# Attention steps of the later tiles one position ahead, and the quarters of the norm's reciprocals at other positions

## The chip, the core and the metric

The kernel runs on one core of a Trainium2 chip. The metric is the time of one execution on the device, in microseconds (us). Before the change it is 1777.77 us, the median of three runs (1776.62 to 1777.86).

A core has TensorE (PE in the profile; its weight loads are PEld), VectorE (DVE), ScalarE (ACT), GpSimd (POOL) and SyncE (SP), which issues the transfers here. Each takes its own instructions in order, and they wait for each other by semaphores.

## The reference

All is float32. An attention over chunks of 64 tokens is followed by two gated layers; the second normalizes its input first.

```python
# q, k, v: (8, 8, 576, 64); chunks of 64 tokens, 9 to a sequence
scores = scale * np.matmul(q_c, k_c.transpose(0, 1, 2, 4, 3))
scores = scores - np.max(scores, axis=-1, keepdims=True)
attn = np.exp(scores)
attn = attn / (np.sum(attn, axis=-1, keepdims=True) + 1e-09)
out = np.matmul(attn, v_c)            # as x: 4608 tokens x 512

g = x @ w_gate                        # layer 1: 512 -> 1536
silu = g * (1.0 / (1.0 + np.exp(-g)))
x = silu * (x @ w_val) @ w_out        # 1536 -> 512

rms = np.sqrt(np.mean(x * x, axis=-1, keepdims=True) + 1e-06)
xn = x / rms * rms_g                  # layer 2, the same with xn
```

## The kernel before

Every product of layer 1 is made of three matmuls on values that are split into a high and a low part (`mm3`, lines 483 to 485): high by high, high by low, low by high. So a tile `x` comes as `xh` and `xl`, a hidden tile as `hh` and `hl`.

**Blocks, iterations, positions.** The tokens form 9 blocks of 512 (0 to 8). In layer 1 a block has 12 iterations, one for each 128 of the 1536 hidden features. An iteration has three stretches on PE of 12 matmuls each: `g` (`emit_g`), `v` (`emit_v`) and `y` (`emit_y`), where `y` multiplies the hidden tile of the iteration before by its output weights. Behind each stretch stands a place for other work, so a block has 36 places, called positions: position 3f is behind `g` of iteration f, 3f + 1 behind `v`, 3f + 2 behind `y`. A table `at` holds what is emitted at each (`put`), counted from a block's start, and the main loop calls `run(0)`, `run(1)`, `run(2)`. Each engine's queue then has its instructions in the order in which they were emitted.

**The chain of a hidden tile.** After `g`, ACT takes the tanh (L495) and DVE makes the product `sg` of the gate (L496, which ends the use of `g`'s PSUM bank). After `v`, DVE multiplies by `v` (L512, which ends the use of `v`'s bank; there is one bank for `g` and one for `v`), ACT rounds to `hh` (L515), and DVE makes `hl` (L517), which `y` of the next iteration needs in its second matmul. In the program L512 of an iteration is emitted ahead of position 3f + 2, L496 behind position 3f, and L517 at the start of the next iteration, ahead of its `g`: on DVE whatever was emitted at position 3f + 2 stands ahead of this `hl`.

**Attention.** There are 36 tiles of 128 tokens (0 to 35); a tile is needed a block after its attention is made. From tile 8 on, the steps of tile i stand around a = `score_at(i)`, counted from the start of block 0, and e = `score_at(i + 1)`:

- at a - 1, `trans_att`: two transpositions on DVE into `qT` and `kT` (L328);
- at a, `att_both(i - 1)`: on PE, the second product of tile i - 1 (16 matmuls, L441, from `pT`) and the scores of tile i (16 matmuls, L345, from `qT` and `kT`), both of 64x64, into the PSUM tile `both`;
- at a + 1 and a + 2, `att_m` and `att_n`: maximum and difference on DVE (L364, L365), exponential on ACT, sum and reciprocal on DVE (L378 to L382), a multiplication on POOL (L383), which makes `p`;
- at e - 4 and e - 3, `att_td`: two halves of a transposition of `p` into `pT` on DVE (L399, eight instructions of 32x128 each);
- at e, `att_both(i)`, and at e + 1, `att_lo(i)`: DVE makes `xl` of the tile (L477).

The loads of the chunks that come later (`load_qk`, `load_v`) are spread over positions that are counted from a - 1.

**The rest in blocks 1 to 8.** The norm of the block before: squares and their sum on POOL (L562 to L568), a sum by PE at position 17 (L586, L587), a square root on ACT, its reciprocal on DVE in four quarters of 128x128 (`rms_rec`, L600), a Newton step at position 27 (L605 to L609) and four multiplications from position 28 on (`rms_x`, L617). From block 1 to the start of block 7 the weights of layer 2 are also converted, one at each of positions 7, 13, 19, 25, 31 and 1 (of the next block): three instructions on DVE, L128, L131 and L136 (the trio, below), then sums and differences on POOL and roundings on ACT (L185 to L191). In the first iteration of a block, DVE and ACT also copy `y` of the block before out of PSUM (L548, L550).

```python
    def score_at(i):
        n = i - 8
        return NP + (8 * n if n < 4 else 32 + 9 * (n - 4))   # NP = 36
```

So from tile 12 on the steps repeat every 9 positions, four tiles to a block: `att_both` stands at positions 5, 14, 23 and 32 of a block, the halves of `att_td` at 1, 2, 10, 11, 19, 20, 28 and 29, and `trans_att` at 4, 13, 22 and 31. The quarters of the reciprocal stand at 19, 21, 23 and 25.

Of the kernel before, what the change touches and what calls it, by code (L numbers as in the profile page):

```python
# [19 lines left out]
def tile_kernel(  # L20
# [270 lines left out]
    def trans_tok(i, tags=None):  # L291
        ts_ = []
        both = ps_pair("a", f"qkP{i}") if tags is None else None
        pts = []
        for z, nm in enumerate("qk"):
            t = tok[i][z]
            if both is None:
                pt = ps.tile([P, HP, P], F32, tag=tags[z], name=f"{nm}P{i}")
            else:
                pt = both[:, z].rearrange("p (h q) -> p h q", h=HP)  # L300
            for hp in range(HP):
                nc.tensor.transpose(
                    pt[:, hp, :], t[:, 2 * hp:2 * hp + 2, :].rearrange("p a b -> p (a b)"), ident
                )
            pts.append(pt)
        for z, nm in enumerate("qk"):
            if i < NW // P:
                sb = spare_tile([P, HP, P], f"{nm}T{i}")
            else:
                sb = att.tile([P, HP, P], F32, tag=f"{nm}T", name=f"{nm}T{i}")  # L310
            nc.scalar.copy(sb, pts[z])
            ts_.append([sb[:, hp] for hp in range(HP)])
        qkT[i] = ts_
# [7 lines left out]
    def trans_att(i):  # L321
        ts_ = []
        for z, nm in enumerate("qk"):
            t = att.tile([P, HP, P], F32, tag=f"{nm}T", name=f"{nm}T{i}")
            tv = t.rearrange("p a (b c) -> p a b c", c=32)
            (g0, n0), (g1, n1) = where[2 * i], where[2 * i + 1]
            if g0 == g1:
                nc.vector.transpose(out=tv, in_=gt[g0][z][:, :, 2 * n0:2 * n0 + 4, :])  # L328
            else:
                nc.vector.transpose(out=tv[:, :, 0:2], in_=gt[g0][z][:, :, 2 * n0:2 * n0 + 2, :])  # L330
                nc.vector.transpose(out=tv[:, :, 2:4], in_=gt[g1][z][:, :, 2 * n1:2 * n1 + 2, :])
            ts_.append([t[:, hp] for hp in range(HP)])
        qkT[i] = ts_
# [22 lines left out]
    def att_m(i):  # L356
        sb = score.pop(i)
        m = att.tile([P, 2, HP], F32, tag="m", name=f"m{i}")
        if i < NW // P:
            pt = spare_tile([P, HP, 2, CH], f"p{i}")  # L360
        else:
            pt = att.tile([P, HP, 2, CH], F32, tag="p", bufs=2, name=f"p{i}")
        s3 = sb.rearrange("p z (h c) -> p z h c", h=HP)
        nc.vector.tensor_reduce(out=m, in_=s3, op=ALU.max, axis=AX.X)  # L364
        nc.vector.tensor_tensor(  # L365
            out=pt.rearrange("p h z c -> p z h c"),
            in0=s3,
            in1=m.rearrange("p z (h o) -> p z h o", o=1).to_broadcast([P, 2, HP, CH]),
            op=ALU.subtract,
        )  # L370
        nc.scalar.activation(pt, pt, AF.Exp, scale=SCALE)
        prob[i] = pt

    def att_n(i):
        pt = prob[i]
        r = att.tile([P, HP * 2, 1], F32, tag="r", name=f"r{i}")
        p8 = pt.rearrange("p a b c -> p (a b) c")
        nc.vector.tensor_reduce(  # L378
            out=r.rearrange("p a o -> p (a o)"), in_=p8, op=ALU.add, axis=AX.X
        )  # L380
        nc.vector.tensor_scalar_add(r, r, 1e-9)
        nc.vector.reciprocal(out=r, in_=r)  # L382
        nc.gpsimd.tensor_tensor(  # L383
            out=p8, in0=p8, in1=r.to_broadcast([P, HP * 2, CH]), op=ALU.mult
        )
# [3 lines left out]
    def att_td(i, c):  # L389
        pt = prob[i]  # L390
        if c == 0:
            probT[i] = att.tile([P, HP, P], F32, tag="pT", name=f"pT{i}")
        pT = probT[i]
        for a in range(2):
            r = (2 * c + a) * 32
            for z in range(2):
                for b in range(2):
                    o = (2 * z + b) * 32
                    nc.vector.transpose(  # L399
                        out=pT[o:o + 32, :, r:r + 32], in_=pt[r:r + 32, :, z, b * 32:b * 32 + 32]  # L400
                    )
# [61 lines left out]
    def att_both(i):  # L463
        both = ps_pair("a", f"both_{i}")
        if i >= 2 * NW // P:
            att_pv(i, i * P // NW, xb=both[:, :, :HP * CH], put_off=True)
        if i + 1 < NT_:
            att_s(i + 1, sb=both[:, :, HP * CH:])
        if i >= 2 * NW // P:
            att_hi(i, i * P // NW)  # L470

    def att_lo(i, j):
        xb = xps.pop(i)
        xh, xl = x_tiles(0, j)
        o = i * P - blocks[j][0]
        ah, al = (t[:, :, o:o + P].rearrange("p h (c q) -> p c h q", c=2) for t in (xh, xl))
        nc.vector.tensor_sub(al, xb, ah.bitcast(F32))  # L477
# [118 lines left out]
    def rms_rec(j, z):  # L596
        n = blocks[j][1] // 4
        ms, r = rms[j]
        a = slice(z * n, (z + 1) * n)
        nc.vector.reciprocal(out=r[:, a], in_=r[:, a])  # L600
# [22 lines left out]
    def tiles_of(j):  # L623
        t0, n = blocks[j]
        return list(range(t0 // P, (t0 + n) // P))
# [4 lines left out]
    NP = 3 * NF  # L630

    def put(l, j, pos, fn):
        at.setdefault((l * NB + j) * NP + pos, []).append(fn)
# [11 lines left out]

    def score_at(i):
        n = i - 8
        return NP + (8 * n if n < 4 else 32 + 9 * (n - 4))

    for x, (l, j) in enumerate(seq):  # L650
        if x + 1 < len(seq):
            nl, nj = seq[x + 1]
            if nl == 0:
                for n, i in enumerate(tiles_of(nj)):
                    if i >= 8:
                        a = score_at(i)
                        e = score_at(i + 1)
                        b = a - 1 - x * NP
                        if i == 8:
                            put(0, 0, a, lambda: att_both(7))  # L660
                        put(0, 0, a - 1, lambda i=i: trans_att(i))
                        put(0, 0, a + 1, lambda i=i: att_m(i))
                        put(0, 0, a + 2, lambda i=i: att_n(i))
                        put(0, 0, e - 4, lambda i=i: att_td(i, 0))
                        put(0, 0, e - 3, lambda i=i: att_td(i, 1))
                        put(0, 0, e, lambda i=i: att_both(i))
                        put(0, 0, e + 1, lambda i=i, nj=nj: att_lo(i, nj))
                    else:
                        b = (0, 9, 18, 27)[n]
                        put(l, j, b, lambda i=i: trans_tok(i))  # L670
                        put(l, j, b + 2, lambda i=i: att_s(i))
                        put(l, j, b + 3, lambda i=i: att_m(i))
                        put(l, j, b + 4, lambda i=i: att_n(i))
                        put(l, j, b + 6, lambda i=i: att_t(i))
                        put(l, j, b + 7, lambda i=i, nj=nj: att_pv(i, nj))
                        put(l, j, b + 8, lambda i=i, nj=nj: att_lo(i, nj))
                    for c in (2 * i, 2 * i + 1):
                        g = where[c][0]
                        if g > 0 and c == groups[g][-1] and g + 2 < len(groups):
                            dq, dv, nq = {4: (21, 18, 10), 7: (3, 9, 12), 8: (8, 12, 12)}.get(i, (1, 11, 8))  # L680
                            spread(l, j, b + dq, nq, lambda g=g: load_qk(g + 2))
                            spread(l, j, b + dv, 3, lambda g=g: load_v(g + 2))
        if x > 0 and seq[x - 1][0] == 0:
            pj = seq[x - 1][1]
            for d in range(KD):
                put(l, j, 3 + 2 * d, lambda pj=pj, d=d: rms_sq(pj, d))
            put(l, j, 14, lambda pj=pj: rms_split(pj))
            put(l, j, 17, lambda pj=pj: rms_mm(pj))
            for z in range(4):
                put(l, j, 19 + 2 * z, lambda pj=pj, z=z: rms_rec(pj, z))  # L690
            put(l, j, 27, lambda pj=pj: rms_newton(pj))
            for d in range(KD):
                put(l, j, 28 + 2 * d, lambda pj=pj, d=d: rms_x(pj, d))
# [286 lines left out]
    with tc.manual_schedule():  # L980
# [151 lines left out]
        pj = NB - 1  # L1132
# [111 lines left out]
```

## Time and profile before

| what | value |
|---|---|
| median of three runs | 1777.77 us |
| the profiled execution's own time | 1777.3 us |
| its span, first to last instruction | 1775.5 us |
| PE busy | 1740.8 us, 98% of the span |
| PEld busy | 1468.2 us, 83% |
| DVE busy | 1260.3 us, 71% |
| ACT busy | 672.4 us, 38% |
| POOL busy | 394.6 us, 22% |
| layer 1, blocks 2 to 7 | from 249.9 to 887.8 us of the span |

The profile is of one execution. A page of it gives the busy time of each engine, a chain of waits and the costliest groups of instructions; the trace behind it can be asked for a stretch (busy time of each engine and PE's granted clock), for the waits of an engine, added up by who ended them, and for the instructions of an engine in order of time. Matmuls overlap: one of 512 columns is shown with 0.39 us, but the next starts sooner, so the time that PE needs is read from start to start. A time in brackets behind an instruction, [1.52 <-DVE hl L517], says how long its engine had been idle before it and what ended that.

### The profile page before, as it was taken

To read this page: it belongs to the slowest core of one execution; us is meant where nothing else is said; L and a number is where in the kernel's file an instruction comes from. 1 tells how busy PE (TensorE), PEld (TensorE's weight loads), DVE (VectorE), ACT (ScalarE), POOL (GpSimd) and SP (SyncE) were. 2 spreads that over 40 slices of the span, in tenths; PEclk is the share of its full clock that TensorE was granted. 3 is DMA by queue.
4 is the path that set the end of the run, shared out by engine and by line. 5 is a ranking of instruction groups with operands and counts; after the bars stand their busy time and mean duration, and the time that the engine had idled before them with its cause. 6 is when DMAs were issued, how large, how long until landed. Compare 5 with 4: busy or idle time off the path is not lost.

```text
span 1775.5 us, 28911 instructions
## 1 busy us (share of the span) xinstructions
PE 1740.8 (98%) x10086; PEld 1468.2 (83%) x10086; DVE 1260.3 (71%) x2250; ACT 672.4 (38%) x1248; POOL 394.6 (22%) x391
## 2 busy tenths in 40 slices
PE   7999999999999999999999999999999999999998
PEld 5788878777788787778888888888888888999998
DVE  6996776977878777785735566955794478568566
ACT  6772323223332332323122334623452345345343
POOL 1002244243342534242031200200120011002000
PEclk8999999999999999999999999999999999999999
DMA  9997777776777766773335476687678768987986
GB/s 218 316 261 198 208 217 198 218 197 203 217 210 215 218 203 203 218 211 126 117 120 202 137 238 195 200 258 218 194 211 247 211 188 223 299 271 226 312 254 177
DMA packets 451457, 379.73 MB, mean 214 GB/s; under 512 B 275696, under 2 KB 302320, under 8 KB 451312
## 3 DMA queue, kind: packets, MB, share of 16 engines
q1 hardware_dynamic: 449712, 377.68, 72.1%
q8 instruction: 81, 1.33, 0.3%
q14 instruction: 64, 0.52, 0.1%
q10 hardware_dynamic: 1600, 0.20, 0.1%
HBM read 316.41 MB, written 61.34 MB: 213 GB/s over the span
## 4 chain that ended last, share of the span: by engine, by line
PE 83%; DVE 8%; SPq 3%; DMA 2%; issue 2%; ACT 1%; POOL 1%; ACTq 0%; DVEq 0%; POOLq 0%
PE g L483 5%; PE g L485 4%; PE g L484 4%; PE v L483 4%; PE v L484 4%; PE v L485 4%; PE y L484 2%; PE y L485 2%; PE y_b L484 2%; PE y_b L483 2%; PE y_b L485 2%; PE y L483 2%; DVE pT L399 2%; SPq L317 2%; PE ygA L484 1%
## 5 line engine op out<-in xcount | busy, mean ns | idle before, releaser
L515 ACT CAST hh<-sg 128x512 fp32r<-128x512 f32 x108 | 67.1, 621 | 375.2 <-DVE sg L512 375.2
L483 PE MATMUL g<-xh,wg 128*128 128x512 f32 x432 | 173.1, 401 | 1.8 <-DVE sg L496 1.1
L483 PE MATMUL v<-xh,wv 128*128 128x512 f32 x432 | 169.9, 393 | 3.7 <-DVE sg L512 2.7
L484 PE MATMUL g<-xl,wg 128*128 128x512 f32 x432 | 169.5, 392 | 0.0
L485 PE MATMUL g<-xh,lg 128*128 128x512 f32 x432 | 169.4, 392 | 0.0
L485 PE MATMUL v<-xh,lv 128*128 128x512 f32 x432 | 168.2, 389 | 0.0
L484 PE MATMUL v<-xl,wv 128*128 128x512 f32 x432 | 168.2, 389 | 0.0
L881 POOL TENSOR_TENSOR h<-h,h 128x512 f32<-128x512 f32 (+1 forms) x30 | 37.1, 1235 | 521.2 <-DVE h L859 521.2
L496 DVE SCALAR_TENSOR_TENSOR sg<-sg,g 128x512 f32<-128x512 f32 x108 | 73.3, 679 | 107.7 <-ACT sg L495 107.7
L399 DVE STREAM_TRANSPOSE pT<-p 32x128 f32<-32x128 f32 x448 | 135.5, 302 | 6.1
L495 ACT ACTIVATE sg<-g 128x512 f32<-128x512 f32 x108 | 64.4, 597 | 168.4 <-PE g L485 167.9
L917 DVE TENSOR_TENSOR hl<-h,hh 128x512 fp32r<-128x512 f32 (+1 forms) x180 | 121.7, 706 | 6.0 <-ACT hh L916 5.9
L916 ACT CAST hh<-h 128x512 fp32r<-128x512 f32 (+1 forms) x180 | 100.4, 577 | 47.2 <-PE yvA L485 20.0
L383 POOL TENSOR_TENSOR p<-p,r 128x512 f32<-128x512 f32 x36 | 40.3, 1121 | 340.7 <-DVE r L382 273.5
L840 DVE TENSOR_TENSOR sgt<-sgt,sig 128x512 f32<-128x512 f32 (+1 forms) x90 | 58.3, 648 | 74.1 <-ACT sig L839 74.0
L839 ACT ACTIVATE sig<-sgt 128x512 f32<-128x512 f32 (+1 forms) x90 | 53.2, 591 | 147.4 <-DVE sgt L847 147.3
L517 DVE TENSOR_TENSOR hl<-sg,hh 128x512 fp32r<-128x512 f32 x108 | 88.0, 815 | 25.8 <-ACT hh L515 24.7
L483 PEld LDWEIGHTS v<-xh,wv 128*128 128x128 f32 x432 | 81.1, 188 | 23.3 <-DVE sg L512 5.2
L483 PEld LDWEIGHTS g<-xh,wg 128*128 128x128 f32 x432 | 81.6, 189 | 21.4 <-DVE sg L496 2.3
L485 PEld LDWEIGHTS g<-xh,lg 128*128 128x128 f32 x432 | 81.6, 189 | 17.5
L484 PEld LDWEIGHTS g<-xl,wg 128*128 128x128 f32 x432 | 81.7, 189 | 16.6 <-DVE xl L477 0.4
L485 PEld LDWEIGHTS v<-xh,lv 128*128 128x128 f32 x432 | 81.1, 188 | 17.1
(806 smaller groups left out, 4684.7 us busy)
## 6 DMA issues: line engine op xcount, KB each, us to landing
wrg<-w_scratch SPq DMA_DIRECT2D x210, 256.0 KB, 3.3
wrv<-w_scratch SPq DMA_DIRECT2D x210, 256.0 KB, 3.4
wro<-w_scratch SPq DMA_DIRECT2D x210, 256.0 KB, 3.2
lg<-lo_scratch SPq DMA_DIRECT2D x96, 256.0 KB, 2.9
lv<-lo_scratch SPq DMA_DIRECT2D x96, 256.0 KB, 3.2
lo<-lo_scratch SPq DMA_DIRECT2D x96, 256.0 KB, 4.0
w_scratch<-wsg SPq DMA_DIRECT2D x42, 256.0 KB, 2.6
w_scratch<-wsv SPq DMA_DIRECT2D x42, 256.0 KB, 2.7
```

Source lines behind the costliest of these rows:

```text
L399: nc.vector.transpose(out=pT[o:o + 32, :, r:r + 32], in_=pt[r:r + 32, :, z, b * 32:b * 32 + 32])
L483: nc.tensor.matmul(o, sh, mh, start=first, stop=False, skip_group_check=free)
L484: nc.tensor.matmul(o, sh, ml, start=False, stop=False, skip_group_check=free)
L485: nc.tensor.matmul(o, sl, mh, start=False, stop=last, skip_group_check=free)
L495: nc.scalar.activation(sg[:, :n], g[:, :n], AF.Tanh, scale=0.5)
L496: return sg, lambda: nc.vector.scalar_tensor_tensor(out=sg[:, :n], in0=sg[:, :n], scalar=1.0, in1=g[:, :n], op0=ALU.add, op1=ALU.mult)
L515: nc.scalar.copy(hh[:, :n], sg[:, :n])
L517: return product, lambda: nc.vector.tensor_sub(hl[:, :n], sg[:, :n], hh[:, :n].bitcast(F32))
L839: nc.scalar.activation(sg[:, :tw], src[:, :tw], AF.Sigmoid)
L840: nc.vector.tensor_mul(t[:, :tw], src[:, :tw], sg[:, :tw])
L916: nc.scalar.copy(hh[:, :tw], src)
L917: nc.vector.tensor_sub(hl[:, :tw], src, hh[:, :tw].bitcast(F32))
```

## The change

From tile 12 on, every step of a tile's attention moves one position ahead: the table's second branch begins at 31 in place of 32. `att_both` then stands at positions 4, 13, 22 and 31, behind `v` in place of behind `y`; the halves of `att_td` at 0, 1, 9, 10, 18, 19, 27 and 28; `trans_att` at 3, 12, 21 and 30; `att_m`, `att_n` and `att_lo` move with them, and so do the spread loads of these tiles. The last steps of tile 11 (`att_td`, `att_both`, `att_lo`), which are counted from the next tile, move too. The quarters of the reciprocal go from 19, 21, 23 and 25 to 20, 21, 23 and 26. Nothing is added or taken away: PE, DVE, ACT and POOL have the same instructions.

```diff
     def score_at(i):
         n = i - 8
-        return NP + (8 * n if n < 4 else 32 + 9 * (n - 4))
+        return NP + (8 * n if n < 4 else 31 + 9 * (n - 4))
...
             for z in range(4):
-                put(l, j, 19 + 2 * z, lambda pj=pj, z=z: rms_rec(pj, z))
+                put(l, j, (20, 21, 23, 26)[z], lambda pj=pj, z=z: rms_rec(pj, z))
```

**DVE, iterations 0 and 1 of a block.** The names carry block and iteration (`hl_5_0` is of block 5, iteration 0; the last number is the program's own). Before:

```order
L496 SCALAR_TENSOR_TENSOR sg_5_0_6531<-sg_5_0_6531,g_5_0_6518 128x512
L399 STREAM_TRANSPOSE pT_6557<-p_6458 32x4x32 x8
L128 TENSOR_SCALAR cmo_1_6570<-w64o_1_6348 128x512
L131 SCALAR_TENSOR_TENSOR cmo_1_6570<-w64o_1_6348,cmo_1_6570 128x512
L136 SCALAR_TENSOR_TENSOR cro_1_6537<-cro_1_6537,cmo_1_6570 128x512
L512 SCALAR_TENSOR_TENSOR sg_5_0_6531<-v_5_0_6541,sg_5_0_6531 128x512
L550 COPY ysb_0_4_6588<-y_4_1_5490 128x512
L550 COPY ysb_0_4_6589<-y_4_b 128x512
L399 STREAM_TRANSPOSE pT_6557<-p_6458 32x4x32 x8
L517 TENSOR_TENSOR hl_5_0_6555<-sg_5_0_6531,hh_5_0_6554 128x512
L496 SCALAR_TENSOR_TENSOR sg_5_1_6630<-sg_5_1_6630,g_5_1_6617 128x512
L328 STREAM_TRANSPOSE qT_6660<-xq_5821 128x512
```

And with the change:

```order
L399 STREAM_TRANSPOSE pT_6537<-p_6436 32x4x32 x8
L496 SCALAR_TENSOR_TENSOR sg_5_0_6535<-sg_5_0_6535,g_5_0_6522 128x512
L399 STREAM_TRANSPOSE pT_6537<-p_6436 32x4x32 x8
L128 TENSOR_SCALAR cmo_1_6582<-w64o_1_6352 128x512
L131 SCALAR_TENSOR_TENSOR cmo_1_6582<-w64o_1_6352,cmo_1_6582 128x512
L136 SCALAR_TENSOR_TENSOR cro_1_6550<-cro_1_6550,cmo_1_6582 128x512
L512 SCALAR_TENSOR_TENSOR sg_5_0_6535<-v_5_0_6554,sg_5_0_6535 128x512
L550 COPY ysb_0_4_6600<-y_4_1_5526 128x512
L550 COPY ysb_0_4_6601<-y_4_b 128x512
L517 TENSOR_TENSOR hl_5_0_6568<-sg_5_0_6535,hh_5_0_6567 128x512
L328 STREAM_TRANSPOSE qT_6636<-xq_5803 128x512
L328 STREAM_TRANSPOSE kT_6638<-xk_5804 128x512
```

The first half of L399 now stands ahead of the gate's product L496, the second half ahead of the trio and no longer between the copies and `hl`; the transpositions L328 (`qT`, then `kT`) now stand straight behind `hl`, where the next L496 stood between before.

**DVE, iteration 6 of a block.** Before:

```order
L496 SCALAR_TENSOR_TENSOR sg_5_6_7137<-sg_5_6_7137,g_5_6_7124 128x512
L399 STREAM_TRANSPOSE pT_7171<-p_7039 32x4x32 x8
L600 RECIPROCAL rr_7107<-rr_7107 128x128
L128 TENSOR_SCALAR cmv_1_7189<-w64v_1_6927 128x512
L131 SCALAR_TENSOR_TENSOR cmv_1_7189<-w64v_1_6927,cmv_1_7189 128x512
L136 SCALAR_TENSOR_TENSOR crv_1_7151<-crv_1_7151,cmv_1_7189 128x512
L512 SCALAR_TENSOR_TENSOR sg_5_6_7137<-v_5_6_7155,sg_5_6_7137 128x512
L399 STREAM_TRANSPOSE pT_7171<-p_7039 32x4x32 x8
L517 TENSOR_TENSOR hl_5_6_7169<-sg_5_6_7137,hh_5_6_7168 128x512
```

And with the change:

```order
L399 STREAM_TRANSPOSE pT_7143<-p_7009 32x4x32 x8
L496 SCALAR_TENSOR_TENSOR sg_5_6_7141<-sg_5_6_7141,g_5_6_7128 128x512
L399 STREAM_TRANSPOSE pT_7143<-p_7009 32x4x32 x8
L128 TENSOR_SCALAR cmv_1_7200<-w64v_1_6931 128x512
L131 SCALAR_TENSOR_TENSOR cmv_1_7200<-w64v_1_6931,cmv_1_7200 128x512
L136 SCALAR_TENSOR_TENSOR crv_1_7164<-crv_1_7164,cmv_1_7200 128x512
L512 SCALAR_TENSOR_TENSOR sg_5_6_7141<-v_5_6_7168,sg_5_6_7141 128x512
L600 RECIPROCAL rr_7111<-rr_7111 128x128
L517 TENSOR_TENSOR hl_5_6_7182<-sg_5_6_7141,hh_5_6_7181 128x512
L328 STREAM_TRANSPOSE qT_7245<-xq_6404 128x512
```

The first quarter of the reciprocal went from ahead of the trio and L512 to behind L512; the second half of L399 went from behind L512 to ahead of the trio.

**PE, iteration 1 of a block.** With the change:

```order
L485 MATMUL v_5_1_6648<-xh_5_5499,lv_5_1_6446 128x512
L441 MATMUL both_6664<-pT_6537,xv_5542 64x64 x16
L345 MATMUL both_6664<-kT_6638,qT_6636 64x64 x16
L483 MATMUL y_5_0_6707<-hh_5_0_6567,wo_0_460 128x512
L484 MATMUL y_5_0_6707<-hl_5_0_6568,wo_0_460 128x512
```

Before, L441 and L345 stood behind the twelve matmuls of `y`; now they stand between `v` and `y`.

## Rows read from the trace of the kernel before

**Rows 1.** Busy time by stage, blocks 2 to 7: start:end, length, engines, PEclk, DMA, GB/s.

```profile
249.00:888.00 639.00, 627.84 (x4114) 510.68 (x4113) 487.44 (x968) 194.13 (x371) 230.88 (x254) 1.00 0.68 198
```

**Rows 2.** Waits of PE in blocks 1 to 7: us in total, times, longest us.

```profile
PE y L484 <- DVE hl L517: 9.6, 7, 1.5
PE v L483 <- DVE sg L512: 2.7, 6, 0.8
PE g L483 <- DVE sg L496: 0.7, 2, 0.4
```

**Rows 3.** PE in time, block 5, iteration 1: start us, us, instruction, [idle before].

```profile
580.45 0.39 PE L483 MATMUL v<-xh,wv 128*128 128x512 f32 x1
...
583.17 0.39 PE L483 MATMUL y<-hh,wo 128*128 128x512 f32 x1
585.08 0.50 PE L484 MATMUL y<-hl,wo 128*128 128x512 f32 x1 [1.52 <-DVE hl L517]
...
587.52 0.40 PE L485 MATMUL y_b<-hh,lo 128*128 128x512 f32 x1
...
588.94 0.50 PE L483 MATMUL g<-xh,wg 128*128 128x512 f32 x1
```

**Rows 4.** PE in time, block 5, iteration 7, last of g and last of y.

```profile
634.19 0.39 PE L485 MATMUL g<-xh,lg 128*128 128x512 f32 x1
...
640.64 0.39 PE L485 MATMUL y_b<-hh,lo 128*128 128x512 f32 x1
```

**Rows 5.** DVE in time, block 5, iterations 0 and 1.

```profile
573.18 0.69 DVE L496 SCALAR_TENSOR_TENSOR sg<-sg,g 128x512 f32<-128x512 f32 x1 [2.99 <-ACT sg L495]
...
578.19 0.68 DVE L512 SCALAR_TENSOR_TENSOR sg<-v,sg 128x512 f32<-128x512 f32 x1
...
581.23 2.52 DVE L399 STREAM_TRANSPOSE pT<-p 32x128 f32<-32x128 f32 x8
583.78 1.24 DVE L517 TENSOR_TENSOR hl<-sg,hh 128x512 fp32r<-128x512 f32 x1
...
585.55 0.70 DVE L328 STREAM_TRANSPOSE qT<-xq 128x512 f32<-128x512 f32 x1
586.18 0.66 DVE L328 STREAM_TRANSPOSE kT<-xk 128x512 f32<-128x512 f32 x1
...
588.10 0.69 DVE L517 TENSOR_TENSOR hl<-sg,hh 128x512 fp32r<-128x512 f32 x1 [0.69 <-ACT hh L515]
```

**Rows 6.** DVE in time, block 5, iterations 6 and 7.

```profile
628.42 0.69 DVE L496 SCALAR_TENSOR_TENSOR sg<-sg,g 128x512 f32<-128x512 f32 x1 [3.43 <-ACT sg L495]
...
631.54 0.95 DVE L600 RECIPROCAL rr<-rr 128x128 f32<-128x128 f32 x1
632.41 0.36 DVE L128 TENSOR_SCALAR cmv<-w64v 128x512 uint32<-128x512 uint32 x1
...
634.21 0.69 DVE L512 SCALAR_TENSOR_TENSOR sg<-v,sg 128x512 f32<-128x512 f32 x1
...
637.49 0.69 DVE L517 TENSOR_TENSOR hl<-sg,hh 128x512 fp32r<-128x512 f32 x1
```

**Rows 7.** PE in time, block 1: a tile's att_both that stands behind v.

```profile
190.22 0.39 PE L485 MATMUL v<-xh,lv 128*128 128x512 f32 x1
190.53 0.69 PE L441 MATMUL both<-pT,xv 64*64 64x64 f32 x32
191.05 0.65 PE L345 MATMUL both<-kT,qT 64*64 64x64 f32 x32
191.63 0.50 PE L483 MATMUL y<-hh,wo 128*128 128x512 f32 x1
```

**Rows 8.** POOL in time, block 5, iteration 1: its first work since block 4.

```profile
578.35 0.74 POOL L185 TENSOR_TENSOR wto<-cro,cro 128x256 f32<-128x256 f32 x1 [8.91 <-DVE cro L136]
```

**Rows 9.** DVE in time, block 5, iteration 2: the trio beside POOL, to the next product.

```profile
594.46 0.80 DVE L128 TENSOR_SCALAR cmg<-w64g 128x512 uint32<-128x512 uint32 x1
...
598.08 0.68 DVE L512 SCALAR_TENSOR_TENSOR sg<-v,sg 128x512 f32<-128x512 f32 x1
```

## The prediction

> **What bounds the kernel now.** I read first the busy time by stage. In blocks 2 to 7 PE is busy 627.84 of 639.00 us [rows 1], so it is the bound and what can be won there is what it waits, not its work; its granted clock is 1.00 of full (2.4 GHz), so nothing is to be won from the clock. Then the waits of PE [rows 2]: three lines stand in blocks 1 to 7. `y` waits for `hl` seven times (six times in blocks 2 to 7, some 1.5 each, and once in block 1), `v` waits six times for the product L512 that frees its bank, `g` twice for L496. All three are released by DVE. Then PE in order of time, to see what one wait costs with the slower start behind it. Twelve matmuls of `v` take 583.17 - 580.45 = 2.72 [rows 3], 0.2267 each. From the first matmul of `y` to its twelfth should take 11 x 0.2267 = 2.49; it takes 587.52 - 583.17 = 4.35. So **iteration 1 of a block loses 1.86**. In iteration 7, from the last of `g` to the last of `y` are 24 matmuls, 5.44; the rows show 640.64 - 634.19 = 6.45 [rows 4]. So **iteration 7 loses 1.01**.
>
> Last, DVE in order of time, to see why it is late. At a block's start it idles 2.99 before L496 (573.18), and then works without a longer pause through half a transposition, the trio, L512, two copies and the other half, which runs from 581.23 to 583.78; only then comes `hl`, until 585.02 [rows 5], while `y` could have used it in its second matmul at 583.40. At iteration 6 it idles 3.43 before L496, then come half a transposition, a quarter of the reciprocal, the trio and L512 at 634.21 [rows 6], while `v` wants its bank at 634.19 + 0.23 = 634.42. So DVE is late at two places of a block and idle just before both. The first loss stands in blocks 2 to 7 (six times), the second in blocks 2 to 6 (five times: the trio at position 19 ends with block 6, and so does the wait).
>
> **The change, part by part.** I replay DVE with the durations of the rows, in the new order, on the old clock of block 5.
>
> *Block start.* The first half of L399 moves ahead of L496, where 2.99 of idle time is free and the half takes 2.5. L496 still starts at 573.18, when ACT has its tanh. Behind it comes the second half, where the first stood, so the trio, L512 (578.19) and the copies stay where they are. `hl` starts at 581.23 in place of 583.78. It takes 0.69 where nothing disturbs it and took 1.24 here [rows 5], so it ends between 581.92 and 582.47, and `y`, which wants it at 583.40 or later, doesn't wait. **1.86 goes, six times: 11.2.**
>
> *What is late next there.* `att_both` now stands ahead of `y` and wants `qT` and `kT`. They follow `hl` on DVE: 586.18 - 585.55 = 0.63 for the first, 0.66 for the second [rows 5], less some 0.07 by which DVE starts ahead of a reported end (0.70 against 0.63). So `kT` is there at 583.14, or at 583.69 behind a slow `hl`. The scores want it at 583.17 + 0.08 (a step of 0.31 in place of 0.23 before L441) + 0.52 = 583.77 [rows 7]. The margin is 0.63, or 0.08. I take no wait, and keep the slow end for a rival.
>
> *Iteration 6.* The first half of L399 moves into the 3.43 of idle time before L496; the second stands behind L496. The quarter of the reciprocal, which held the trio back from 631.54 to 632.41, moves behind L512. So the trio starts at 631.54, 0.87 earlier, and L512 at 633.34. It ends at 634.03, 0.39 before `v` wants the bank. Behind L512 stand the quarter, until 634.8, and the cast on ACT, some 0.7 behind the product's end (0.69 before the undisturbed `hl` [rows 5]); `hl` runs from 634.8 to 635.5, and `y` wants it at 637.4. `kT` is there at 636.7, and wanted at 637.74 (634.42, the 2.72 of `v`, and 0.60 as above). **1.01 goes, five times: 5.05.**
>
> *`att_both` behind `v`.* A tile of block 1 whose step already stands there costs 191.63 - 190.22 - 0.23 = 1.18 [rows 7]; behind `y` it costs 588.94 - 587.52 - 0.23 = 1.19 [rows 3]. Nothing.
>
> *Block 1.* It holds what is left of [rows 2]: one wait of `g` at iteration 9 for L496 behind the Newton step, one at iteration 7, and one each of `v` and `y` in iteration 10. The half transposition moves there too, but the Newton step stays. I take about half of the two waits of `g` with their slow starts: **0.5**. Bounds: nothing, and all of them, 0.8 + 0.7 + 0.5 and three slow starts of 0.34 (1.86 less the 1.52 of the wait [rows 3]), 3.0.
>
> *Loads, POOL, the other quarters.* The spread loads go one position ahead with their tiles on SP's queue. PE waits for no transfer in these blocks [rows 2], and the transfers are no more; nothing. POOL's multiplication of `p` moves with L382, its distance to L399 stays three positions; were POOL late, the half transposition would hold L496 up, and `g` wants its bank only behind `v` and `y`, 5.44 later. The other quarters stay or go back by one position, to places where DVE next waits for PE; the Newton step comes one position behind the last in place of two, with the same 5.44 for `g`'s bank behind it. Nothing.
>
> **The sum.** 11.2 + 5.05 + 0.5 = 16.7. Against the profiled execution, 1777.3, that is 1760.6; the median of the runs is 0.5 above it, so **1761.0**. A measurement of this kernel can tell about 0.2%, 3.6 us, from no change.
>
> **A rule against it.** `hl` took 1.24 beside POOL in place of 0.69 [rows 5], and POOL starts a run of work behind the trio, at 578.35, with 0.74 an operation [rows 8]. The Trainium skill, page "SBUF — State Buffer", section "SBUF: two separate sides", says that VectorE with two SBUF inputs and GpSimd take a shared port pair as an exclusive lock for a whole instruction, the other fully blocked. By that `hl` could take 0.69 + 0.74 = 1.43 (an estimate from that page and the rows); the trace shows less, 1.24. By the rule `kT` would come 0.11 late, with a slow start 0.45 a block, and the sum would be 14.0, which gives 1763.8; it is one way into the first rival below.
>
> **The rivals.**
>
> *The wait moves to `kT`.* If copies and `hl` come as little as 0.1 later than replayed with a slow `hl`, the scores wait in iteration 1. For it: the margin of 0.08. Against: `hl` 2.55 earlier meets POOL at another operation. Price: up to the 0.55 that a slow `hl` adds, and a slow start of 0.34, so 0.9 in six blocks, 5.3: up to 1766.3; with half of the 0.55, 3.7 and 1764.7.
>
> *Iteration 7 keeps its wait.* The margin of `v`'s bank is 0.39. If the trio starts that much later, because the half transposition does not fit before L496, the five waits stay: 5.05, so 1766. Against: 3.43 of idle time for 2.5.
>
> *The wait only changes its name.* If DVE's idle time before L496 can't be used, since `p` is not ready one position earlier, all stays as late as it is: 1777. Against: POOL makes `p` three positions ahead.
>
> *Slower: the trio meets POOL.* In iteration 2 the trio takes 598.08 - 594.46 = 3.62 beside POOL [rows 9], in iteration 6 only 634.21 - 632.41 = 1.80 [rows 6]. If the new order lets POOL's work fall on the trio of iterations 0 and 6, each is 1.82 longer: `kT` comes at 583.69 + 1.82 = 585.51, 1.74 late and with a slow start 2.1; L512 ends at 635.85, 1.43 late, with a slow start 1.8. That is 3.9 a block for the 2.87 that goes: five times 1.0 and 0.2 in block 7, so some 5 slower, 1782.5. It decides once the trio is longer by about 1.3 at both places (kT late by 1.2 and the bank by 0.9, with two slow starts 2.8). Against: POOL is idle for 8.91 until that trio's own L136 releases it [rows 8].
>
> **How the numbers follow.** The forecast 0.72, `kT` 0.14, iteration 7 0.07: all faster, 0.93. The wait that changes its name 0.04: same. The trio 0.03: slower. The likeliest is 1761.0. The forecast's own range is 1758.5 (all of block 1's waits gone, 2.5 more) to 1763; the range that holds the first three cases reaches up to 1766.5, and leaves out 0.07.
>
> **What would show it.** In blocks 2 to 7 the waits of `y` for `hl` and of `v` for L512 are gone, a block takes 2.9 less, and PE is idle under 2 us in these blocks in place of 11 [rows 1]. In DVE's time, L399 stands in the idle time before L496, and `hl` starts some 2.5 earlier after its block's first `g`. The forecast is wrong where a new line stands among PE's waits, `both` for `kT` above all, or where L399 waits for `p`; and if the waits are gone but the time isn't, then PE's steps behind them got slower.

## The result, and the profile after

| what | before | with the change |
|---|---|---|
| median of five runs | 1777.77 us (1775.93 to 1779.22) | 1760.82 us (1760.48 to 1761.69) |
| the profiled execution's own time | 1777.3 us | 1761.0 us |
| its span | 1775.5 us | 1759.2 us |

The ratio of the times, changed to before, is 0.9907, with a 95% interval from 0.9892 to 0.9921: 0.9% faster, about 17 us.

The first line of the page, with the changed kernel's busy times (share of the span, instructions):

```profile
PE 1737.4 (99%) x10086; PEld 1470.9 (84%) x10086; DVE 1264.0 (72%) x2250; ACT 674.3 (38%) x1248; POOL 393.2 (22%) x391
```

No engine has less to do; PE's share rose from 98% to 99% because the span is shorter. Blocks 2 to 7 now go from 249.05 to 870.91 us. Their busy times by stage, with the columns of [rows 1]:

```profile
249.00:871.00 622.00, 622.00 (x4110) 510.74 (x4110) 489.00 (x967) 195.25 (x370) 227.66 (x253) 1.00 0.71 203
```

PE is busy in 622.00 of 622.00 us; in [rows 1] it was idle for 11.16. PE's waits over the whole run hold no line of blocks 2 to 7. Of the three lines of [rows 2], two are left, both in block 1, and `y` for `hl` is gone:

```profile
PE v L483 <- DVE sg L512: 0.9, 1, 0.9
...
PE g L483 <- DVE sg L496: 0.7, 1, 0.7
```

DVE in order of time, block 5, iterations 0 and 1, answers to [rows 5]. The first `g` of this block starts at 560.23 here, at 569.57 before:

```profile
559.70 2.50 DVE L399 STREAM_TRANSPOSE pT<-p 32x128 f32<-32x128 f32 x8
563.84 0.69 DVE L496 SCALAR_TENSOR_TENSOR sg<-sg,g 128x512 f32<-128x512 f32 x1 [1.64 <-ACT sg L495]
564.56 2.53 DVE L399 STREAM_TRANSPOSE pT<-p 32x128 f32<-32x128 f32 x8
...
568.99 0.68 DVE L512 SCALAR_TENSOR_TENSOR sg<-v,sg 128x512 f32<-128x512 f32 x1
...
571.33 0.69 DVE L550 COPY ysb<-y_b 128x512 f32<-128x512 f32 x1 [1.06 <-ACT ysb L548]
571.94 0.68 DVE L517 TENSOR_TENSOR hl<-sg,hh 128x512 fp32r<-128x512 f32 x1
...
573.16 0.67 DVE L328 STREAM_TRANSPOSE kT<-xk 128x512 f32<-128x512 f32 x1
...
577.70 1.40 DVE L517 TENSOR_TENSOR hl<-sg,hh 128x512 fp32r<-128x512 f32 x1
```

`hl` starts 11.71 behind the block's first `g`, where it started 14.21 behind it before: 2.50 earlier, one half of L399. The other half, at 559.70, fills idle time ahead of L496: 1.64 of it is left. The same iteration on PE answers to [rows 3]:

```profile
573.92 0.69 PE L441 MATMUL both<-pT,xv 64*64 64x64 f32 x32
574.44 0.65 PE L345 MATMUL both<-kT,qT 64*64 64x64 f32 x32
575.02 0.50 PE L483 MATMUL y<-hh,wo 128*128 128x512 f32 x1
575.36 0.39 PE L484 MATMUL y<-hl,wo 128*128 128x512 f32 x1
```

The scores start at 574.44, and `kT` was there at 573.16 + 0.67 = 573.83: a margin of 0.61. `y` finds `hl` long done. Iteration 6, to be held against [rows 6]:

```profile
617.23 0.69 DVE L496 SCALAR_TENSOR_TENSOR sg<-sg,g 128x512 f32<-128x512 f32 x1 [1.01 <-ACT sg L495]
617.95 2.53 DVE L399 STREAM_TRANSPOSE pT<-p 32x128 f32<-32x128 f32 x8
620.51 0.43 DVE L128 TENSOR_SCALAR cmv<-w64v 128x512 uint32<-128x512 uint32 x1
...
622.38 0.68 DVE L512 SCALAR_TENSOR_TENSOR sg<-v,sg 128x512 f32<-128x512 f32 x1
622.98 0.94 DVE L600 RECIPROCAL rr<-rr 128x128 f32<-128x128 f32 x1
623.83 0.63 DVE L517 TENSOR_TENSOR hl<-sg,hh 128x512 fp32r<-128x512 f32 x1
```

L512 ends at 623.06; `v` of iteration 7 starts at 623.22 without a wait:

```profile
623.22 0.39 PE L483 MATMUL v<-xh,wv 128*128 128x512 f32 x1
```

**Where the 16.3 us of the span came from.** I measure a block from its first `g` matmul to the next block's. Blocks 2 to 6 take 103.73 in place of 106.57: 2.85 less each, 14.25. Block 7 takes 103.24 in place of 105.07: 1.83. Block 1 takes 107.35 in place of 107.85: 0.50. Block 1 starts 0.33 earlier, and what follows block 7 takes 0.58 more. Of the latter, block 8, where the quarters move too, takes 98.43 in both; layer 2 and what stands ahead of block 1 are not touched by the change. I take both for the spread between executions. 14.25 + 1.83 + 0.50 + 0.33 - 0.58 = 16.33.

### The profile page after: what moved, and what is told of

Read it like the earlier page. It is cut to its first block, busy times and chain, and to the rows that moved or that the text cites. A ratio compares the mean times of both kernels' runs of the same rounds, so it can differ in the third digit from the quotient of the medians.

```text
span 1759.2 us, 28904 instructions
## 1 busy us (share of the span) xinstructions
PE 1737.4 (99%) x10086; PEld 1470.9 (84%) x10086; DVE 1264.0 (72%) x2250; ACT 674.3 (38%) x1248; POOL 393.2 (22%) x391
## 4 chain that ended last, share of the span: by engine, by line
PE 92%; DVE 4%; DMA 1%; issue 1%; ACT 1%; POOL 1%; SPq 1%; DVEq 0%; POOLq 0%; ACTq 0%
PE g L483 5%; PE g L484 5%; PE g L485 5%; PE v L483 5%; PE v L485 5%; PE v L484 5%; PE y L483 3%; PE y L485 3%; PE y L484 3%; PE y_b L485 3%; PE y_b L483 3%; PE y_b L484 3%; PE ygA L484 1%; PE yvA L485 1%; PE ygA L485 1%; PE yvA L483 1%
## 5 line engine op out<-in xcount | busy, mean ns | idle before, releaser
L399 DVE STREAM_TRANSPOSE pT<-p 32x128 f32<-32x128 f32 x448 | 135.5, 302 | 6.2
L496 DVE SCALAR_TENSOR_TENSOR sg<-sg,g 128x512 f32<-128x512 f32 x108 | 73.1, 677 | 85.7 <-ACT sg L495 85.6
L512 DVE SCALAR_TENSOR_TENSOR sg<-v,sg 128x512 f32<-128x512 f32 x108 | 74.2, 687 | 37.6 <-PE v L485 36.0
```

Source lines behind the costliest of these rows:

```text
L399: nc.vector.transpose(out=pT[o:o + 32, :, r:r + 32], in_=pt[r:r + 32, :, z, b * 32:b * 32 + 32])
L496: return sg, lambda: nc.vector.scalar_tensor_tensor(out=sg[:, :n], in0=sg[:, :n], scalar=1.0, in1=g[:, :n], op0=ALU.add, op1=ALU.mult)
L512: nc.vector.scalar_tensor_tensor(out=sg[:, :n], in0=vv[:, :n], scalar=0.5, in1=sg[:, :n], op0=ALU.mult, op1=ALU.mult)
```

## The experiments

Two theories were put to the test. **Theory A**, the prediction's: what counts is DVE's order, what stands ahead of `hl` (iteration 1) and ahead of L512 (iteration 7). **Theory B**, the rival: what counts is PE's order. `att_both`, now ahead of `y`, keeps PE busy for some 1.2 before `y` asks for `hl`, and that hides most of a wait of 1.5. Both can explain the same lines of the profile, so the two orders were changed apart. The diffs of `td_only`, `td_kept` and `rec_only` are against the kernel before, the others against the changed one. Every ratio is to the kernel before, run beside it (medians 1777.61 for the first four experiments, 1778.84 for the last four).

**td_only: DVE's order changed, PE's kept.** The table stays at 32, and only the halves of L399 move ahead (here those of tiles 8 to 10 as well, which the change leaves), beside the quarters.

```diff
-                        put(0, 0, e - 4, lambda i=i: att_td(i, 0))
-                        put(0, 0, e - 3, lambda i=i: att_td(i, 1))
+                        put(0, 0, e - 5, lambda i=i: att_td(i, 0))
+                        put(0, 0, e - 4, lambda i=i: att_td(i, 1))
...
-                put(l, j, 19 + 2 * z, lambda pj=pj, z=z: rms_rec(pj, z))
+                put(l, j, (20, 21, 23, 26)[z], lambda pj=pj, z=z: rms_rec(pj, z))
```

> The change with the old table (32), but the halves of L399 one position ahead (e - 5, e - 4) and the new places of the reciprocal: att_both, trans_att, att_m and att_n stand where they stood. Theory A (DVE's order ahead of hl is what counts): hl of iteration 0 starts some 2.5 earlier, before y wants it, without the 1.18 of att_both ahead of y; all of the gain, 1761 to 1763 (block 1 may keep a wait). Theory B (att_both between v and y covers the wait): the waits of y for hl stay in part, 1768 or more.

Measured: 1762.85, ratio 0.9918 (0.9905 to 0.9932), which overlaps the change's. PE has no wait in blocks 2 to 7, and a block takes 103.97, 0.24 more than with the change (in iteration 10, 9.58 in place of the 9.34 before). In DVE's time (block 5, first `g` at 562.52) `hl` starts 11.71 behind it, as with the change:

```profile
574.23 0.68 DVE L517 TENSOR_TENSOR hl<-sg,hh 128x512 fp32r<-128x512 f32 x1
```

So the gain, but for that 0.24 a block, needs no new place for `att_both`, for the scores or for any load.

**td_kept: PE's order changed, the halves kept.** The table goes to 31 and the quarters move, and with the table the other attention steps on DVE; but the halves of L399 stay where they stood in the block (from tile 11 on; those of tiles 8 to 10, in block 1, go one position back).

```diff
-        return NP + (8 * n if n < 4 else 32 + 9 * (n - 4))
+        return NP + (8 * n if n < 4 else 31 + 9 * (n - 4))
...
-                        put(0, 0, e - 4, lambda i=i: att_td(i, 0))
-                        put(0, 0, e - 3, lambda i=i: att_td(i, 1))
+                        put(0, 0, e - 3, lambda i=i: att_td(i, 0))
+                        put(0, 0, e - 2, lambda i=i: att_td(i, 1))
...
-                put(l, j, 19 + 2 * z, lambda pj=pj, z=z: rms_rec(pj, z))
+                put(l, j, (20, 21, 23, 26)[z], lambda pj=pj, z=z: rms_rec(pj, z))
```

> The change, but the halves of L399 stay where they stood (e - 3, e - 2 from the new table): everything else moves. Theory A: hl of iteration 0 still ends at 585.02 of block 5's clock, kT behind it at 586.24, wanted by att_both at 583.77: 2.5 late and with a slow start 2.8 in place of 1.86, so 0.95 more in six blocks, 5.7; iteration 7 waits for kT too, 1.3 in place of 1.01: in all slower than before, 1784 to 1790. Theory B (att_both ahead of y covers 1.18 of the wait): faster than before, 1770 to 1775.

Measured: 1786.69, ratio 1.0054 (1.0037 to 1.0071), slower than before: even the fastest of its four times, 1783.46, lies above the slowest before, 1779.39. PE's waits in blocks 2 to 7 (L330 is the transposition of a tile whose two chunks were loaded in different groups):

```profile
PE both L345 <- DVE kT L328: 11.2, 8, 1.5
PE both L345 <- DVE kT L330: 3.4, 3, 1.3
PE both L441 <- DVE pT L399: 1.4, 6, 0.2
```

DVE in order of time, block 3, whose first `g` is at 361.50:

```profile
372.46 0.69 DVE L550 COPY ysb<-y_b 128x512 f32<-128x512 f32 x1 [1.06 <-ACT ysb L548]
373.17 2.53 DVE L399 STREAM_TRANSPOSE pT<-p 32x128 f32<-32x128 f32 x8
375.73 0.69 DVE L517 TENSOR_TENSOR hl<-sg,hh 128x512 fp32r<-128x512 f32 x1
```

With the half still between the copies and `hl`, `hl` starts 14.23 behind `g`, as before, and `kT` behind it comes too late for scores that are wanted sooner: six waits in iteration 1, five in iteration 7. Theory B falls: `att_both` ahead of `y` does not hide the wait, it takes it over.

**rec_only: the quarters alone.**

```diff
-                put(l, j, 19 + 2 * z, lambda pj=pj, z=z: rms_rec(pj, z))
+                put(l, j, (20, 21, 23, 26)[z], lambda pj=pj, z=z: rms_rec(pj, z))
```

> The kernel before with the reciprocal's quarters at 20, 21, 23 and 26 alone. Theory A: iteration 1 keeps its 1.86; in iteration 7 v's wait goes, but the quarter and half of L399 now both stand between L512 and hl, which starts at 637.45 where y wants it done by 637.37: y waits 0.8 with a slow start 1.0. Nothing won, 1776 to 1778. If the quarters are a gain by themselves: 5.05 less, 1772.7.

Measured: 1777.57, ratio 1.0000 (0.9991 to 1.0009), no change. PE's waits in blocks 2 to 7, and the place in iteration 7 on DVE and on PE:

```profile
PE y L484 <- DVE hl L517: 12.7, 11, 1.5
```

```profile
634.11 2.53 DVE L399 STREAM_TRANSPOSE pT<-p 32x128 f32<-32x128 f32 x8
636.65 0.95 DVE L600 RECIPROCAL rr<-rr 128x128 f32<-128x128 f32 x1
637.52 0.63 DVE L517 TENSOR_TENSOR hl<-sg,hh 128x512 fp32r<-128x512 f32 x1
```

```profile
638.20 0.50 PE L484 MATMUL y<-hl,wo 128*128 128x512 f32 x1 [0.72 <-DVE hl L517]
```

`v`'s wait is gone, and `y` waits 0.72 instead: the quarter now stands between L512 and `hl`, behind the second half of L399, which is still there. Iteration 7 takes 10.36, as before the edit.

**rec_old: everything but the quarters.**

```diff
-                put(l, j, (20, 21, 23, 26)[z], lambda pj=pj, z=z: rms_rec(pj, z))
+                put(l, j, 19 + 2 * z, lambda pj=pj, z=z: rms_rec(pj, z))
```

> The change with the reciprocal's quarters at their old positions 19, 21, 23 and 25. Theory A: the first quarter holds the trio and L512 of iteration 6 until 634.21 again, v waits for its bank some 0.5 with a slow start 0.7 in five blocks: 3.5 of the gain lost, 1764.5. If the quarters' places count for nothing, 1761; if they are all of iteration 7's wait, 1766.

Measured: 1763.84, ratio 0.9925 (0.9912 to 0.9937). PE's waits in blocks 2 to 7:

```profile
PE v L483 <- DVE sg L512: 2.6, 5, 0.5
```

Blocks 2 to 6 take 104.52 in place of 103.73, five times 0.79 = 4.0. The edges of the two intervals overlap, so that this is slower than the change is read from the blocks, not from the medians. Of the 1.01 that iteration 7 gained, then, 0.8 needs the quarter's new place; and that place alone gives nothing. Most of the other 0.2 shows in the kernel before behind the wait of `v`: the first matmul of `y` stood at 637.85, and the second followed 0.39 later in place of 0.23, as `hl` ended at 637.49 + 0.69 = 638.18 [rows 6]. That short wait goes once the half is moved: in `rec_old` the second matmul of `y` follows the first without it.

```profile
638.24 0.50 PE L484 MATMUL y<-hl,wo 128*128 128x512 f32 x1
```

**copy3: a known delay ahead of `hl`.** The second of DVE's two copies in a block's first iteration is made three times.

```diff
-                nc.vector.tensor_copy(s[d][:, :w], y[:, :w])
+                for _ in range(3 if d == 3 else 1):
+                    nc.vector.tensor_copy(s[d][:, :w], y[:, :w])
```

> The changed kernel, with DVE's second copy of y out of PSUM (L550) made three times over, the same values to the same place: some 1.3 to 1.4 more on DVE ahead of hl, qT and kT at each block's start. Nothing is left out. Theory A (the margins of the replay are real: hl is done over 0.8 before y wants it and more with att_both ahead, kT 0.6 before the scores want it): y still doesn't wait, but the scores wait for kT 0.7 to 0.8 and with a slow start 1.0 to 1.1 in six blocks, so 6 to 7 slower than the change, 1767 to 1768. If DVE has room to spare there, 1761 to 1762; if hl is what bounds it, y and not the scores waits.

Measured: 1768.63, ratio 0.994 (0.9925 to 0.9955). DVE in block 5 (first `g` at 565.54; lines behind the edit have one more):

```profile
576.65 2.14 DVE L551 COPY ysb<-y_b 128x512 f32<-128x512 f32 x3 [1.06 <-ACT ysb L548]
578.70 0.92 DVE L517 TENSOR_TENSOR hl<-sg,hh 128x512 fp32r<-128x512 f32 x1
...
580.18 0.66 DVE L328 STREAM_TRANSPOSE kT<-xk 128x512 f32<-128x512 f32 x1
```

and what PE waits for in iteration 1 of block 5:

```profile
580.90 0.69 PE L345 MATMUL both<-kT,qT 64*64 64x64 f32 x32 [0.97 <-DVE kT L328]
```

`kT` starts 580.18 - 565.54 = 14.64 behind `g`, 1.71 later than with the change (573.16 - 560.23 = 12.93); expected were 1.3 to 1.4, but the copies took 1.45 more, and `hl` 0.92 in place of 0.68. Iteration 1 grows from 9.48 to 10.67, by 1.19. So 0.5 of the 1.71 was hidden, near the margin of 0.61 that the trace showed, and what is late next is `kT`, not `hl`.

**one_more and one_back: the same edit by another position.** The table at 30, then at 33.

```diff
-        return NP + (8 * n if n < 4 else 31 + 9 * (n - 4))
+        return NP + (8 * n if n < 4 else 30 + 9 * (n - 4))
```

> The change with 30 in the table: every attention step one more position ahead, att_both behind g (positions 3, 12, 21, 30), the second half of L399 at position 0, kT at position 2, ahead of hl. Theory A: the waits of y for hl and of v for L512 stay away; kT is wanted 2.72 earlier than with 31 and stands behind the copies, at about the time at which it is wanted, so some waits come back, at most 1.8 in six blocks: 1762 to 1772. If 31 is the only place that works, 1777.

Measured: 1763.82, ratio 0.9917 (0.9901 to 0.9933). Blocks 2 to 6 take 103.71 and have no waits, as with 31: the waits for `kT` that were expected in six blocks did not come, and the time lies in the expected range for another reason. Block 1 takes 110.71 in place of 107.35. DVE there:

```profile
228.82 2.52 DVE L399 STREAM_TRANSPOSE pT<-p 32x128 f32<-32x128 f32 x8
231.38 1.19 DVE L606 SCALAR_TENSOR_TENSOR ms<-ms,rr 128x512 f32<-128x512 f32 x1
232.59 1.09 DVE L609 SCALAR_TENSOR_TENSOR rr<-ms,rr 128x512 f32<-128x512 f32 x1
233.61 0.68 DVE L496 SCALAR_TENSOR_TENSOR sg<-sg,g 128x512 f32<-128x512 f32 x1
```

A half of L399 and the Newton step stand together ahead of L496, and the `g` that follows waits 2.71 for its bank. What PE then does is told in the last section.

```diff
-        return NP + (8 * n if n < 4 else 31 + 9 * (n - 4))
+        return NP + (8 * n if n < 4 else 33 + 9 * (n - 4))
```

> The change with 33 in the table: every attention step two positions later, att_both behind g (6, 15, 24, 33), the halves of L399 at 2 and 3, 20 and 21. Theory A: no half stands between the trio and L512 or ahead of the copies any more, so L512 and the copies come some 2.5 earlier at a block's start and hl, behind one half, is done at about 583.1 where y wants it by 583.4; iteration 6 likewise; a wait may come in iteration 11, where L617 stands. 1764 to 1772, so faster than before as well. If the gain came from being earlier as such, 1777 or more.

Measured: 1779.33, ratio 1.0002 (0.9992 to 1.0012): no change from before, and a miss. Its longest line among PE's waits in blocks 2 to 7, and DVE in block 5 (first `g` at 571.35):

```profile
PE g L483 <- DVE sg L496: 8.3, 15, 1.0
```

```profile
583.46 1.27 DVE L517 TENSOR_TENSOR hl<-sg,hh 128x512 fp32r<-128x512 f32 x1
584.77 2.53 DVE L399 STREAM_TRANSPOSE pT<-p 32x128 f32<-32x128 f32 x8
587.33 0.69 DVE L496 SCALAR_TENSOR_TENSOR sg<-sg,g 128x512 f32<-128x512 f32 x1
...
637.11 2.52 DVE L399 STREAM_TRANSPOSE pT<-p 32x128 f32<-32x128 f32 x8
639.64 0.95 DVE L600 RECIPROCAL rr<-rr 128x128 f32<-128x128 f32 x1
640.52 0.63 DVE L496 SCALAR_TENSOR_TENSOR sg<-sg,g 128x512 f32<-128x512 f32 x1
```

Here `hl` starts 12.11 behind `g`, and `y` no longer waits for it, as expected. But the second half, behind `hl`, now stands ahead of L496, and DVE is still behind from the copies: L496 starts at 587.33, and PE's next `g` waits 0.24. The longer waits of this kind stand where something else lies between the half and L496: 0.72 behind a quarter of the reciprocal (L496 at 640.52), and up to 1.04 behind a multiplication of the norm (L617). Up to three such waits in a block, 15 in all, and `kT`'s in iteration 11 gave back what the two old ones cost.

**newton_later: what is left in block 1.** The Newton step and the multiplications behind it go one position back.

```diff
-            put(l, j, 27, lambda pj=pj: rms_newton(pj))
+            put(l, j, 28, lambda pj=pj: rms_newton(pj))
...
-                put(l, j, 28 + 2 * d, lambda pj=pj, d=d: rms_x(pj, d))
+                put(l, j, 29 + 2 * d, lambda pj=pj, d=d: rms_x(pj, d))
```

> The changed kernel with the Newton step at position 28 in place of 27 and the four multiplications at 29, 31, 33 and 35. Theory A: what is left of block 1's waits (g for L496 in iteration 7, v for L512 and the scores for kT in iteration 10, 1.7 together by PE's waits) comes from the Newton step ahead of the halves of L399; some of it goes: 1759 to 1760.5. If not, 1761.

Measured: 1761.63 (1759.6 to 1762.2), ratio 0.9901 (0.9887 to 0.9915). In the profile block 1 takes 105.70 in place of 107.35, as L496 now stands ahead of the Newton step and iteration 10 has no wait. The 1.65 is 0.1% of the time, and the times don't tell it from the change. None of these runs is faster than the change by more than a measurement can tell.

## Why the prediction was right

The forecast was 1761.0, and the time 1760.82. Its steps, one by one:

- **The sum.** The profiled execution fell by 16.3 where 16.7 was forecast, the median by 16.95. That the two medians lie only 0.2 apart is in part luck; what the runs bear out is the terms.
- **What bounds the kernel.** PE's waits for DVE, not PE's work: with the waits gone PE has no idle time left in blocks 2 to 7. Shown by the stage's row, and by `td_only`, which leaves PE's order alone.
- **Iteration 1, 1.86 six times.** `hl` was to start 11.66 behind `g` and started 11.71 behind it. Block 7, which has this loss alone, gave 1.83. That it was the half of L399 ahead of `hl` is shown by `td_kept` (half kept, `hl` late as before, loss kept under another name). One reading of the old rows was wrong, without weight in the sum: DVE does pause in that stretch, 1.06 ahead of its second copy, which waits for ACT's copy (L548), before as after.
- **The slower start of 0.34.** In [rows 3] the wait of 1.52 is counted from the reported end of the matmul before, 583.17 + 0.39 = 583.56, while the next was due at 583.40. So 0.16 of the 0.34 lies in the counting, and PE's steps behind the wait took only 0.18 longer. The 1.86 is read from start to start and stands.
- **`kT`'s margin, 0.63 or 0.08.** It is 0.61: `hl` took 0.68 and not 1.24, so the slow end did not come. `copy3` used the margin up and turned 1.71 of delay into 1.19 of loss, so the first rival named the right next wait; it was only not reached.
- **Iteration 7, 1.01 five times.** Gone, but with less to spare than replayed: L512 ended 0.16 before `v` started, where 0.39 was predicted, since from L496 to the trio it took 620.51 - 617.23 = 3.28 in place of 631.54 - 628.42 = 3.12, and the trio 1.87 in place of 1.80. `rec_old` shows what stands on it: with the quarter back in its old place the wait returns, five times 0.79.
- **Block 1, 0.5.** The size came out as 0.50, by luck more than by working. It was to be half of `g`'s two waits. In fact the `g` behind iteration 9 lost its wait (the iteration fell by 0.60), the one behind iteration 7 waits longer (0.46 more), and iterations 10 and 11 fell by 0.38 together. The first two come from the quarters: with the quarters alone (`rec_only`) iterations 7 and 9 take 9.05 and 8.16 as with the change, and without them (`rec_old`) 8.59 and 8.77 as before.
- **`att_both` behind `v`, nothing.** It costs 1.18 there (573.61, the last matmul of `v`, to 575.02, less 0.23), as predicted.
- **`g`'s bank with 5.44 to spare, nothing.** In blocks 2 to 7 it held for this change; in block 1 the quarter that moved behind L512 of iteration 6 put L496 of iteration 7 back by 0.48, and the next `g` waits 0.73 in place of 0.27. As a general step it was too simple: it counts from the time DVE would start if it were on time. `one_back` stands a half of L399 ahead of an L496 that is late already, and `g` waits; `one_more` does so beside the Newton step, and `g` waits 2.71.
- **The rule on the shared port.** `hl` of iteration 0 starts when POOL is idle and takes 0.68; the slow one is now iteration 1's, 577.70, with 1.40, where `y` is far from wanting it. POOL's operation ahead of it runs from 577.52 to 578.55. By the rule cited in the prediction (the Trainium skill, page "SBUF — State Buffer", section "SBUF: two separate sides") `hl` would wait for that end and then take 0.69, until 579.24, an estimate from the page and the rows; it ended at 579.10. So the trace ended 0.14 sooner than the rule there, and the collision has moved to where it costs nothing.
- **The rival that the wait only changes its name.** In the profiled execution of the change no L399 waits for `p`, so the idle time ahead of L496 could be used.
- **The slower rival.** The trio of iterations 0 and 6 met no POOL operation: in iteration 6 it takes 622.38 - 620.51 = 1.87, against 1.80 in [rows 6] and the 3.62 that the rival needed.

## What to carry to other kernels

When the bounding engine waits for another one that is idle shortly before, look for work on that engine that is ready early but stands between the late value and its producer, and move that work alone: here the halves of a transposition, with the quarters of a reciprocal, carried the gain, and the matmuls that moved with them could have stayed. Where two items hold up the same stretch, moving one can leave the wait or pass it to the next consumer: in iteration 7 `rec_only` passed it from `v` to `y`, and `rec_old` left it at `v`. And a consumer that moves ahead, as the scores in `td_kept`, takes a wait over that stays. Before another position is tried, replay the queue from where the engine really is, its lateness included, not from where it should be.

## What was not expected of the hardware

**PE's clock fell to half behind some waits.** In `one_more`, busy time by stage in block 1 (PEclk is third from the end), and PE in order of time:

```profile
231.40:234.30 2.90, 0.23 (x2) 0.00 (x0) 2.87 (x4) 0.00 (x0) 1.74 (x2) 1.00 0.61 147
234.30:237.60 3.30, 3.26 (x8) 2.58 (x9) 3.30 (x5) 1.24 (x3) 1.01 (x2) 0.50 0.54 172
```

```profile
234.34 0.79 PE L483 MATMUL g<-xh,wg 128*128 128x512 f32 x1 [2.71 <-DVE sg L496]
234.94 0.63 PE L484 MATMUL g<-xl,wg 128*128 128x512 f32 x1
235.36 0.63 PE L485 MATMUL g<-xh,lg 128*128 128x512 f32 x1
```

After a wait of 2.71 the granted clock is 0.50, the level of 1.2 GHz, for 3.3 us, and matmuls start 0.427 apart in place of 0.227. The iteration that begins with them takes 11.18 in place of 9.48, so the wait costs 1.7 more than itself, where the slower start behind a wait was 0.34 in the prediction. In `td_kept` the same happened behind `kT`'s wait in blocks 3, 6 and 7, whose iteration 1 takes 13.1 to 13.2, but not in blocks 2, 4 and 5, where it takes 11.5 to 11.6 after waits of like length (1.05 and 1.26 in both groups). Block 3:

```profile
377.70:378.40 0.70, 0.70 (x33) 0.63 (x33) 0.60 (x2) 0.00 (x0) 0.00 (x0) 1.00 0.29 46
378.40:382.00 3.60, 3.60 (x10) 2.81 (x11) 3.50 (x5) 2.29 (x6) 2.50 (x4) 0.55 0.42 108
```

There PE had run `att_both` in pieces, with idle stretches of 0.23 and 1.26, before the clock fell. The waits of 1.5 in the kernel before never brought it: its clock is 1.00 in all of blocks 2 to 7 [rows 1]. What decides between blocks 2 and 3 of `td_kept` these runs don't settle. In block 1 of `td_kept`, behind a wait of 2.44 for `kT` in iteration 10, the granted clock was 0.50 from 239.40 to 243.00, and matmuls started 0.427 apart until 245.29: that iteration took 16.18, where it took 11.36 before. In the profiled execution of `td_kept`, whose span is 14.0 longer than before's, the three blocks at half clock account for some 4.8, and block 1, where the wait grew as well, for 3.8. This execution is the slowest of the four, 1791.33; with 1788.35, 1785.03 and 1783.46 their mean granted clocks were 0.991, 0.993, 0.995 and 0.996. So the spread of `td_kept` goes with the clock, and its fastest time, 5.9 above the kernel before at the same clock, is the nearest that these runs have to what the waits alone cost.
